# Last batch of a two-layer mixture: seven block products instead of eight for the second layer too, on two units at once

## The chip, the core and the metric

One core of one Trainium2 chip runs the kernel. The metric is device time of a whole execution in microseconds (us); the median of three runs of the kernel before is 1190.45 us (1190.12 to 1192.12). TensorE (PE) multiplies, VectorE (DVE), ScalarE (ACT) and GpSimd (POOL) do the element work, SyncE (SP) and ScalarE issue the DMAs used here. [...]

## The reference, cut to what matters

```python
scores = q @ k.T / sqrt(D)                 # 4 batches, 8 heads, 768 rows, D = 64
scores += -slope[h] * dist                 # local window of n_local = 96 and n_global = 8 first columns
a = softmax(where(keep, scores, -1e9)) ; x = a @ v      # x: 3072 rows x 512
p = domain_probs / domain_probs.sum(-1)    # 4 domains
for e in range(4):
    h = maximum(x @ w1[e], 0)              # 512 -> 1024
    out += p[:, e:e+1] * (h @ w2[e])       # 1024 -> 512
```

## The kernel before

A batch is 768 rows (six tiles of 128, or two halves of 384). The hidden columns of the four domains are cut into units of 256: `units` (line 700) lists (batch, domain, group), 16 units a batch, 64 in all. Each fp32 operand is kept as two fp32r parts, a high part (a ScalarE copy) and a low part (the value minus the high part), and each product is three matmuls: high by high, high by low, low by high.

For each unit `first(i)` (line 815) makes the hidden values. The product of w1 with x is done by seven products of 2 x 2 blocks (Strassen in Winograd's form): `product` (line 782) issues six matmuls of 384 columns into one PSUM bank of the pool `ps_mm` (four banks). VectorE adds the partial sums, ScalarE does relu and writes the high part of h, and VectorE writes the low part. `second(i)` (line 876) multiplies h with w2: for each of six row tiles six matmuls of 512 columns into one bank, then one VectorE instruction weights the tile with the mixture's probability and adds it to `acc`. At the last unit of a batch ScalarE's queue sends `acc` out.

The order of a batch (from line 944) is first(0), then first(i), second(i-1) for each i, and at last second(15). Attention for the next batch (`attention`) is put between these as steps, so that its last steps end ahead of the batch's last second but one; the blocks of the next x (`blocks`, line 607) are then made by ScalarE, VectorE and GpSimd beside the following products. The last batch has no attention beside it. `load_w1` and `load_w2` (lines 720, 760) run as chores: in batch 0 they load raw weights, make the block sums and both parts with GpSimd and ScalarE and keep them in device memory; in later batches SP's queue fetches the parts back, two buffers each.

From line 941 the order is written out by hand up to a few steps into batch 0 (`Ordered.on`, class at line 30). After that the program's planner places each engine's instructions by its own estimate of their times, with program order as priority; each engine executes its own list in order.

Of the kernel before, what the change touches and what calls it, by code (L numbers as in the profile page):

```python
# [2 lines left out]

# [22 lines left out]
def f32(ap):  # L26
    return ap.bitcast(F32)
# [159 lines left out]
def attn_moe_kernel(ctx: ExitStack, tc, q, k, v, n_global, n_local, domain_probs, w1, w2, out):  # L187
# [9 lines left out]
    HALF = S // 2  # L197
    TPH = HALF // P
    SCALE = 1.0 / math.sqrt(D)

    const = ctx.enter_context(tc.tile_pool(name="const", bufs=1))
    ident = const.tile([P, P], F32, name="ident")
# [2 lines left out]
    ng = load_int(nc, const, n_global, "ng")  # L205

    main = ctx.enter_context(ExitStack())
    ve, ac, po, sy, te = (Ordered(tc, e) for e in (nc.vector, nc.scalar, nc.gpsimd, nc.sync, nc.tensor))

    PAIRS = (0, 2, 1, 3)  # L210
# [7 lines left out]
    HELDSTEPS = 14  # L218

    PL = P + NGLOB  # L220
    fast = main.enter_context(tc.tile_pool(name="fast", bufs=1))

# [48 lines left out]
    NT = N // P  # L271
    prob = const.tile([P, NT, E], F32, name="prob")

    xp = main.enter_context(tc.tile_pool(name="xp", bufs=1))
    wp = main.enter_context(tc.tile_pool(name="wp", bufs=2))
    rp = main.enter_context(tc.tile_pool(name="rp", bufs=1))

    class Pools:


        def __init__(self, stack, name, st, kd, qd, nat, natv, pb, ps, pt, px, early):
            self.early = early

            def sbuf(part, bufs):
                return stack.enter_context(tc.tile_pool(name=f"{name}_{part}", bufs=bufs))
# [427 lines left out]
            sy.dma_start(f32(kept[key]), f32(dst))  # L713

    def fetch(name, key, shape, view):
        dst = wp.tile(shape, F32R, name=name)
        sy.dma_start(f32(dst), f32(kept[key]))
        return view(dst)

# [39 lines left out]

    def load_w2(i, lead=7):  # L760

        if i >= len(units):
            return
        b, e, g = units[i]
# [7 lines left out]
        dst = wp.tile([P, 2, 2, DM], F32R, name="w2s")  # L772
# [5 lines left out]
        waiting[(i, 2)] = (e, g, 2), dst  # L778

    hs = {}  # L780

# [147 lines left out]
        mix = mixture()  # L929
        next(mix)  # L930
    Ordered.on = False
    hp = main.enter_context(tc.tile_pool(name="hp", bufs=2))
    op = main.enter_context(tc.tile_pool(name="op", bufs=1))
    ps_mm = main.enter_context(tc.tile_pool(name="ps_mm", bufs=4, space=PSUM))
    A = Pools(main, "att", st=1, kd=1, qd=1, nat=1, natv=1, pb=2, ps=2, pt=2, px=0, early=False)

    per = E * NPR
    count, span = NPAIR * (6 + NQT) + 5, (13 * per - 12) * 0.97  # L940
    Ordered.on = True
    chores.append(last)
    work_chores()
    for b in range(B):
        att = attention(b + 1, A) if b + 1 < B else iter(())
        emitted = done = 0
        begin = ONSTEPS if b == 0 else 0
        events = [(first, b * per)]
        for i in range(b * per + 1, (b + 1) * per):
            events += [(first, i), (second, i - 1)]  # L950
        events.append((second, (b + 1) * per - 1))
        for n, (fn, i) in enumerate(events):
            if n == len(events) - 2 and b + 1 < B:
                for _ in att:
                    pass
                chores.append(blocks(b + 1))
            if b == 0 and n == 0:
                chores += [load_w2(1, 12), load_w1(2, 6, 3)]
            else:
                chores.append(load_w1(i + 2, 9) if fn is first else load_w2(i + 2))  # L960
            for _ in fn(i):
                work_chores()
                done += 1
                if b == 0 and done == ONSTEPS:
                    next(mix, None)
                    next(att)
                    Ordered.on = False
                    po.held = True
                if b == 0 and done == HELDSTEPS:
                    po.held = False  # L970
                while emitted < count and emitted * (span - begin) < (done - begin) * count:
                    next(att, None)
                    emitted += 1

    main.close()


# [39 lines left out]
```

## Time and profile before

| | |
|---|---|
| median of three runs | 1190.45 us |
| span of the profiled execution (the page gives its span alone) | 1189.2 us |
| TensorE matmul / VectorE / ScalarE / GpSimd busy | 1164.3 / 825.8 / 494.4 / 210.7 us |
| batch 0, 1, 2, 3 by TensorE's order | 85 to 345, to 625, to 919, to 1184 us |

Busy time of an engine is the union of its records. [...] In the time order one line merges neighbouring instructions of one kind: start, length from the first start to the last end, engine, operation, tiles, shape and count; in brackets the idle time ahead and what ended it.

### The profile page before, as it was taken

How to read it: one execution, taken by the hardware profiler on the slowest of the kernel's cores; microseconds unless marked ns; L12 is line 12 of the kernel's file. 1: busy time of each engine (PE TensorE's matmuls, PEld its weight loads, DVE VectorE, ACT ScalarE, POOL GpSimd, SP SyncE). 2: the span in 40 equal slices, each digit the busy share in tenths (PEclk: the TensorE clock that was granted, in tenths of full speed). 3: DMA queues.
4: the chain of work that ended last, by engine and by line, in shares of the span. 5: the costliest groups of instructions: out<-in, count | busy, mean ns of one | idle time of the engine just before them, and what ended most of it. 6: DMA issues, size and time to landing. Idle time of an engine off the chain costs nothing.

```text
span 1189.2 us, 18091 instructions
## 1 busy us (share of the span) xinstructions
PE 1164.3 (98%) x6624; PEld 1039.9 (87%) x6624; DVE 825.8 (69%) x1859; ACT 494.4 (42%) x1268; POOL 210.7 (18%) x221
## 2 busy tenths in 40 slices
PE   7789999999999999999999999999999999999998
PEld 5579899898989898998988998989988999999996
DVE  7887676776687666666758867666666766666665
ACT  7955655565533444444432444444444211111110
POOL 4755665555230000000001000000001000000000
PEclk9999999999999999999999999999999999999999
DMA  8486897878578566666657657575654645554532
GB/s 200 160 246 243 306 299 264 258 278 298 178 244 275 186 209 198 201 217 213 183 178 242 237 198 219 164 238 192 206 186 154 234 188 195 195 187 177 186 133 91
DMA packets 122703, 251.38 MB, mean 211 GB/s; under 512 B 83184, under 2 KB 91376, under 8 KB 106224
## 3 DMA queue, kind: packets, MB, share of 16 engines
q1 hardware_dynamic: 118864, 243.87, 61.8%
q10 hardware_dynamic: 3744, 6.30, 1.4%
q8 instruction: 54, 0.88, 0.3%
q14 instruction: 41, 0.34, 0.1%
HBM read 174.11 MB, written 52.43 MB: 190 GB/s over the span
## 4 chain that ended last, share of the span: by engine, by line
PE 90%; DMA 3%; ACT 3%; DVE 2%; POOL 1%; issue 1%; SPq 0%; POOLq 0%; DVEq 0%
PE pm L43 80%; PE pt L43 6%; PE ps L43 3%; DMA qd<-st_q 2%; ACT pb L43 1%; DVE pb L43 1%; DMA raw<-in_moe_w_dram 1%; POOL w1s L43 0%; DMA q<-in_q_dram 0%; ACT xT L43 0%; ACT pT L43 0%; SPq L43 0%; DVE x L43 0%; ACT w1s L43 0%; POOL w2s L43 0%
## 5 line engine op out<-in xcount | busy, mean ns | idle before, releaser
L43 PE MATMUL pm<-w2s,h 128*128 128x512 f32 x2304 | 551.6, 393 | 1.5 <-DVE h L43 1.5
L43 PEld LDWEIGHTS pm<-w2s,h 128*128 128x128 f32 x2304 | 426.1, 188 | 89.4 <-DVE h L43 3.1
L43 DVE SCALAR_TENSOR_TENSOR acc<-pm,prob,acc 128x512 f32<-128x512 f32 x360 | 267.8, 749 | 151.6 <-PE pm L43 149.7
L43 PE MATMUL pm<-xT,w1s 128*128 128x384 f32 x1536 | 296.0, 337 | 1.7 <-DVE vv L43 1.0
L43 PEld LDWEIGHTS pm<-xT,w1s 128*128 128x128 f32 x1536 | 266.3, 188 | 5.2 <-issue 1.7
L43 PE MATMUL pm<-xB,w1s 128*128 128x384 f32 x1146 | 225.2, 338 | 0.2 <-DVE xB L43 0.2
L43 PEld LDWEIGHTS pm<-xB,w1s 128*128 128x128 f32 x1146 | 200.4, 188 | 5.1 <-issue 0.5
L43 ACT ACTIVATE h<-pm 128x384 fp32r<-128x384 f32 x256 | 124.7, 491 | 176.5 <-DVE pm L43 172.8
L43 DVE SCALAR_TENSOR_TENSOR h<-pm,h 128x384 fp32r<-128x384 f32 x256 | 140.5, 551 | 10.9 <-ACT h L43 7.7
L43 ACT ACTIVATE pb<-pb,nmax 128x256 f32<-128x256 f32 (+1 forms) x192 | 93.8, 495 | 92.1 <-DVE nmax L43 91.2
L43 ACT COPY p<-pm 128x384 f32<-128x384 f32 x63 | 30.2, 479 | 185.8 <-PE pm L43 176.9
L43 POOL COPY vg<-v 32x768 f32<-32x768 f32 x16 | 13.5, 843 | 505.5 <-DMA v<-in_v_dram 440.4
L43 DVE TENSOR_TENSOR u<-pm,p 128x384 f32<-128x384 f32 x64 | 35.6, 557 | 71.2 <-PE pm L43 58.1
L43 DVE CUSTOM_DVE_ANT_0 pb<-ps,nbias 128x256 f32<-128x256 f32 (+1 forms) x192 | 71.5, 396 | 8.3 <-PE ps L43 4.8
L43 ACT COPY pT<-pt 128x512 f32<-128x512 f32 (+1 forms) x96 | 53.4, 556 | 53.6 <-PE pt L43 53.4
L43 DVE TENSOR_TENSOR pm<-pm,vv 128x384 f32<-128x384 f32 x128 | 71.6, 560 | 1.5 <-PE pm L43 1.3
L43 ACT ACTIVATE pb<-pb,zsum 128x256 f32<-128x256 f32 (+1 forms) x144 | 63.3, 484 | 17.9 <-DVE zsum L43 17.8
L43 PE MATMUL pt<-ident,pb 128*128 128x128 f32 x352 | 57.4, 278 | 7.7 <-DVE pb L43 5.4
L43 PEld LDWEIGHTS pt<-ident,pb 128*128 128x128 f32 x352 | 42.1, 141 | 17.8 <-ACT pb L43 3.3
L43 DVE TENSOR_TENSOR vv<-pm,u 128x384 f32<-128x384 f32 x64 | 35.6, 557 | 27.3 <-PE pm L43 26.9
L43 DVE TENSOR_TENSOR u<-pm,u 128x384 f32<-128x384 f32 x64 | 35.6, 557 | 27.1 <-PE pm L43 26.5
L43 POOL TENSOR_TENSOR w2s<-raw,w2s 128x512 fp32r<-128x512 f32 x32 | 40.9, 1293 | 44.8 <-ACT w2s L43 44.7
(91 smaller groups left out, 881.3 us busy)
## 6 DMA issues: line engine op xcount, KB each, us to landing
w1s<-kept SPq DMA_DIRECT2D x48, 1792.0 KB, 7.3
w2s<-kept SPq DMA_DIRECT2D x48, 1024.0 KB, 4.8
kept<-w1s SPq DMA_DIRECT2D x16, 1792.0 KB, 7.9
qd<-st_q SPq DMA_DIRECT2D x96, 192.0 KB, 5.0
raw<-in_moe_w_dram SPq DMA_DIRECT2D x32, 512.0 KB, 4.7
kept<-w2s SPq DMA_DIRECT2D x16, 1024.0 KB, 6.6
v<-in_v_dram SPq DMA_DIRECT2D x16, 384.0 KB, 4.0
out_dram<-acc ACTq DMA_DIRECT2D x24, 256.0 KB, 3.4
```

The source lines that it names most:

```text
L43: ins = fn(*args, **kwargs)
```

## The change

In the last batch alone the products with w2 are done by seven products of blocks as well. Two units (the pair i, i+1 of one domain) are taken together: the contraction of 512 is two blocks of 256 (one 128-column block from each unit), the 512 output columns are two blocks of 256, the rows are two halves of 384. A product is 18 matmuls of 256 columns: three row tiles, two units, three parts. The partial sums of a pair stay in six PSUM banks, X and Y for three row tiles, into whose halves products are added by TensorE, and VectorE adds between them (`behind`). Two banks (`psF`) are left for the w1 products.

`first_late` makes hidden values as whole fp32 blocks in SBUF (`hf`), without high and low parts; `sum_values` (GpSimd) makes four sums of these blocks, and `split_value` (ScalarE and VectorE) and `split_sum` (ScalarE and GpSimd) write the parts. In `period` each of the seven w2 products of a pair is followed by two w1 products of the pair after it; `last_period` has w2 products alone. All of this stands in program order. The first unit's w1 products of the last batch move ahead of the last w2 products of batch 2.

The four sums of w2's blocks (T1 to T4) are made once for each (domain, group) by the chore `load_t` in batches 1 and 2 and kept in device memory. Pools that end before the last batch stand on the other side of SBUF (`mid`), so that the new pools can take their place.

```diff
@@ load_w2: returns for the last batch; w2s comes from its own pool wp2
+    def load_t(e, g, lead=6):
+        raw = rp.tile([P, 2, DM], F32, name="raw2")
+        sy.held = True
+        sy.dma_start(raw, w2[e, g * 2 * P : (g + 1) * 2 * P, :].rearrange("(a p) m -> p a m", p=P))
+        sy.held = False
+        for _ in range(lead):
+            yield 1
+        b11, b12, b21, b22 = (raw[:, f, s] for f in range(2) for s in (slice(0, HM), slice(HM, DM)))
+        low = rp.tile([P, 4, 2, P], F32, name="sums").rearrange("p n a f -> p n (a f)")
+        high = rp.tile([P, KT, 2 * P], F32, name="raw1")
+        po.tensor_sub(low[:, 0], b12, b11)
...
+        ac.copy(high.bitcast(F32R), low)
+        yield 1
+        po.tensor_tensor(low.bitcast(F32R), low, high, op=ALU.subtract)
+        for _ in range(4):
+            yield 1
+        dst = kept[(e, g, 3)] = dp.tile([4, P, 2, HM], F32R, name=f"kept_{e}_{g}_3")
+        for n, src in enumerate((high, low)):
+            ac.dma_start(f32(dst[:, :, n, :]).rearrange("n p m -> p n m"), src)
@@ after the start
+    SLOTS = (
+        ("P1", "A11", "B11", 0, 0), ("P2", "A12", "B21", 0, 0), ("P6", "S2", "T2", 1, 0), ("P5", "S1", "T1", 0, 1),
+        ("P7", "S3", "T3", 1, 1), ("P3", "S4", "B22", 0, 1), ("P4", "A22", "T4", 1, 0),
+    )
+    def first_late(i):
+        def prod(a, x):
+            return product(i, a, x, lt["psF"].tile([P, 512], F32, name="pf"))[:, :HALF]
+        def last(name, pm, other):
+            ve.tensor_add(pm, pm, other)
+            ac.activation(hf[:, HBLOCKS.index(name)], pm, AF.Relu)
+        ac.copy(p1, prod("A11", "B11"))
+        yield
+        last("A11", prod("A12", "B21"), p1)
+        yield
+        ve.tensor_add(u, prod("S2", "T2"), p1)
+        yield
+        ve.tensor_add(vv, prod("S1", "T1"), u)
+        yield
+        pm = prod("S3", "T3")
+        ve.tensor_add(u, pm, u)
+        last("A22", pm, vv)
+        yield
+        last("A12", prod("A22", "T4"), u)
+        yield
+        last("A21", prod("S4", "B22"), vv)
+        yield
+    def halves(eng, dst, k, src):
+        ac.copy(dst[:, 0, k], src)
+        eng.tensor_tensor(dst[:, 1, k], src, f32(dst[:, 0, k]), op=ALU.subtract)
+    def sum_values(i, eng=po):
+        eng.tensor_add(s1, a21, a22)
+        eng.tensor_sub(s2, s1, a11)
+        po.tensor_sub(s4, a12, s2)
+        po.tensor_sub(s3, a11, a21)
+        def big(G, s, pm):
+            for t in range(TPH):
+                n = 0
+                for k in range(2):
+                    for hi, wi in ((0, 0), (1, 0), (0, 1)):
+                        te.matmul(
+                            pm[low][t][:, cols], blk[a][:, hi, k, t * P : (t + 1) * P], w[:, k, wi, :],
+                            start=(n == 0 and name in ("P1", "P6", "P5")), stop=(n == 5), skip_group_check=True,
+                        )
+                        n += 1
+                yield
+            load_late()
+        def behind(s, t, pm, saved, other):
+            X, Y = pm[0][t], pm[1][t]
+            if s == 0:
+                ac.copy(saved[t], X[:, left])
+            elif s == 2:
+                ve.tensor_add(saved[t], Y[:, left], saved[t])
+            elif s == 3:
+                ve.tensor_add(X[:, right], X[:, right], saved[t])
+                ac.copy(other[t], X[:, right])
+            elif s == 4:
+                ve.tensor_add(Y[:, left], Y[:, right], saved[t])
+                ve.tensor_add(Y[:, right], Y[:, right], other[t])
+        def period(G, before):
+            for s in range(7):
+                for _ in big(G, s, pm):
+                    pass
+                if s == 0:
+                    split_value("A12", i + 1)
+                    split_value("A22", i, True)
+                    sum_values(i + 1)
+                    if before:
+                        mix(G - 1, before[1], 3)
+                        mix(G - 1, before[1], 4)
+                elif s == 1:
+                    split_sum("S2", i + 1)
+                    split_sum("S1", i + 1)
+                    if before:
+                        mix(G - 1, before[1], 5)
+                    split_value("A22", i + 1)
+                    split_value("A11", j, True)
...
+                elif s == 6:
+                    split_sum("S3", j, True)
+                    split_sum("S4", j, True)
+                    for t in range(TPH):
+                        mix(G, pm[0], t)
+                for t in range(TPH):
+                    behind(s, t, pm, saved, other)
+                next(more)
+                if final and s == 6:
+                    mix(G, pm[1], 3)
+                next(more)
+        def last_period(G, before):
...
+            for t, _ in enumerate(big(G, 2, pm)):
+                behind(2, t, pm, saved, other)
+            for t in range(TPH):
+                mix(G, X, t, 0)
+            for t, _ in enumerate(big(G, 3, pm)):
+                behind(3, t, pm, saved, other)
...
@@ the loop over batches
-    for b in range(B):
+    for b in range(B - 1):
...
+        tail = b == B - 2
+        if tail:
+            events.append((first_late, (b + 1) * per))
         events.append((second, (b + 1) * per - 1))
...
+            if b in (1, 2) and fn is first and i % 2 == b - 1:
+                chores.append(load_t(*units[i][1:]))
...
+    Ordered.on = True
+    mid.close()
+    late_batch()
```

## Rows read from the trace of the kernel before

**Rows 1.** The page: span, busy time of each engine (share of the span) and instructions, and TensorE's granted clock in tenths for 40 equal slices.
```profile
span 1189.2 us, 18091 instructions
PE 1164.3 (98%) x6624; PEld 1039.9 (87%) x6624; DVE 825.8 (69%) x1859; ACT 494.4 (42%) x1268; POOL 210.7 (18%) x221
PEclk9999999999999999999999999999999999999999
```

**Rows 2.** Busy time by stage: the start's end, batches 0, 1, 2 and 3. Columns: window, its length, busy time of each engine and instructions, granted clock, share of the DMA engines' time, GB/s.
```profile
core 0: us, PE busy (x) PEld busy (x) DVE busy (x) ACT busy (x) POOL busy (x), PEclk, DMA share, GB/s
60.00:85.00 25.00, 21.72 (x130) 18.02 (x129) 20.42 (x47) 14.51 (x32) 14.91 (x15) 1.00 0.76 208
85.00:345.00 260.00, 259.52 (x1507) 233.99 (x1506) 180.10 (x390) 149.90 (x377) 140.51 (x139) 1.00 0.78 270
345.00:625.00 280.00, 279.05 (x1609) 252.01 (x1608) 192.52 (x416) 114.67 (x302) 3.30 (x4) 1.00 0.64 206
625.00:919.00 294.00, 293.29 (x1685) 264.94 (x1685) 207.02 (x438) 123.25 (x318) 10.55 (x8) 1.00 0.62 203
919.00:1189.00 270.00, 264.43 (x1320) 238.20 (x1319) 177.77 (x293) 41.98 (x84) 2.85 (x2) 0.99 0.49 177
```

**Rows 3.** The last link of the chain that ended last (start, length, engine, tile, count), and from the table of waits of 919 to 1189 us, TensorE's only row (in total, times, longest).
```profile
918.78 264.67 PE pm L43 x1320
...
PE pm L43 <- DVE h L43: 0.3, 1, 0.3
```

**Rows 4.** TensorE in order of time in the last batch, one unit.
```profile
980.83 8.36 PE L43 MATMUL pm<-w2s,h 128*128 128x512 f32 x36
989.03 1.23 PE L43 MATMUL pm<-xB,w1s 128*128 128x384 f32 x6
990.10 3.28 PE L43 MATMUL pm<-xT,w1s 128*128 128x384 f32 x18
993.22 2.24 PE L43 MATMUL pm<-xB,w1s 128*128 128x384 f32 x12
```

**Rows 5.** TensorE in order of time in batch 1, with attention's scores (256 columns) and transposes (128 columns) between; then the weight loads of the scores grouped by form.
```profile
402.01 0.64 PE L43 MATMUL ps<-kd,qd 128*128 128x256 f32 x4
402.48 1.21 PE L43 MATMUL pm<-xT,w1s 128*128 128x384 f32 x6
...
406.65 0.64 PE L43 MATMUL ps<-kd,qd 128*128 128x256 f32 x4
407.12 0.60 PE L43 MATMUL pt<-ident,pb 128*128 128x128 f32 x4
407.48 4.81 PE L43 MATMUL pm<-w2s,h 128*128 128x512 f32 x20
...
L43 PEld LDWEIGHTS ps<-kd,qd 128*128 128x128 f32 x288 | 43.9, 188 | 4.9 <-issue 1.2 <-DMA qd<-st_q 0.9
```

**Rows 6.** Groups of instructions over the span, kept apart by form: busy us, mean ns of one, idle before them.
```profile
L43 DVE SCALAR_TENSOR_TENSOR acc<-pm,prob,acc 128x512 f32<-128x512 f32 x360 | 267.8, 749 | 151.6 <-PE pm L43 149.7
L43 ACT ACTIVATE h<-pm 128x384 fp32r<-128x384 f32 x256 | 124.7, 491 | 176.5 <-DVE pm L43 172.8
L43 DVE CUSTOM_DVE_ANT_0 pb<-ps,nbias 128x256 f32<-128x256 f32 x160 | 63.2, 418 | 6.3 <-PE pt L43 3.5 <-PE ps L43 2.8
L43 POOL TENSOR_TENSOR w2s<-raw,w2s 128x512 fp32r<-128x512 f32 x32 | 40.9, 1293 | 44.8 <-ACT w2s L43 44.7
L43 DVE TENSOR_TENSOR vv<-pm,u 128x384 f32<-128x384 f32 x64 | 35.6, 557 | 27.3 <-PE pm L43 26.9
L43 POOL TENSOR_TENSOR sums<-raw 128x256 f32<-128x256 f32 x32 | 23.5, 751 | 37.4 <-DMA raw<-in_moe_w_dram 37.3
L43 ACT COPY pT<-pt 128x256 f32<-128x256 f32 x16 | 6.0, 372 | 0.3 <-PE pt L43 0.3
L43 POOL TENSOR_TENSOR xB<-x,xB 128x384 fp32r<-128x384 f32 x4 | 4.0, 1002 | 1.0 <-ACT xB L43 1.0
L43 ACT CAST xT<-x 128x384 fp32r<-128x384 f32 x8 | 3.9, 512 | 2.4 <-DVE x L43 2.4
L43 DVE TENSOR_TENSOR xT<-x,xT 128x384 fp32r<-128x384 f32 x3 | 1.7, 559 | 1.3 <-ACT xT L43 1.2
```

**Rows 7.** VectorE and GpSimd in order of time at the end of batch 1: a split of 768 columns by VectorE beside two by GpSimd. The same split by VectorE alone is the last of [rows 9].
```profile
631.38 2.63 DVE L43 TENSOR_TENSOR xT<-x,xT 128x768 fp32r<-128x768 f32 x1
...
629.57 3.64 POOL L43 TENSOR_TENSOR xB<-x,xB 128x768 fp32r<-128x768 f32 x2
```

**Rows 8.** DMA issues: count, KB each, median us from issue to landing.
```profile
w1s<-kept SPq DMA_DIRECT2D x48, 1792.0 KB, 7.3
w2s<-kept SPq DMA_DIRECT2D x48, 1024.0 KB, 4.8
```

**Rows 9.** TensorE and VectorE in order of time at the start of the last batch.
```profile
918.78 16.62 PE L43 MATMUL pm<-w2s,h 128*128 128x512 f32 x72 [0.28 <-DVE h L43]
935.23 1.23 PE L43 MATMUL pm<-xB,w1s 128*128 128x384 f32 x6
...
926.30 0.94 DVE L43 TENSOR_TENSOR xT<-x,xT 128x768 fp32r<-128x768 f32 x1
927.17 2.21 DVE L43 SCALAR_TENSOR_TENSOR acc<-pm,prob,acc 128x512 f32<-128x512 f32 x3
929.30 0.95 DVE L43 TENSOR_TENSOR xT<-x,xT 128x768 fp32r<-128x768 f32 x1
```

**Rows 10.** The end: VectorE's last instruction.
```profile
1183.47 0.75 DVE L43 SCALAR_TENSOR_TENSOR acc<-pm,prob,acc 128x512 f32<-128x512 f32 x1 [0.61 <-PE pm L43]
```

More of the change, by code (lines that the diff above doesn't have):

```diff
@@ L2 @@
 from contextlib import ExitStack
+from functools import partial
 import concourse.bass as bass
@@ L220, in attn_moe_kernel @@
     PL = P + NGLOB
-    fast = main.enter_context(tc.tile_pool(name="fast", bufs=1))
+    fast = mid.enter_context(tc.tile_pool(name="fast", bufs=1, side="right"))
     nbias = fast.tile([P, H, 3 * P], BF16, name="nbias")
@@ L715, in fetch @@
     def fetch(name, key, shape, view):
-        dst = wp.tile(shape, F32R, name=name)
+        dst = (wp if name == "w1s" else wp2).tile(shape, F32R, name=name)
         sy.dma_start(f32(dst), f32(kept[key]))
@@ L760, in load_w2 @@
     def load_w2(i, lead=7):
-        if i >= len(units):
+        b, e, g = units[i]
+        if b == B - 1:
             return
-        b, e, g = units[i]
         if b > 0:
@@ L771, in load_w2 @@
             yield 1
-        dst = wp.tile([P, 2, 2, DM], F32R, name="w2s")
+        dst = wp2.tile([P, 2, 2, DM], F32R, name="w2s")
         wts[(i, 2)] = dst
@@ L931, in attn_moe_kernel @@
     Ordered.on = False
-    hp = main.enter_context(tc.tile_pool(name="hp", bufs=2))
     op = main.enter_context(tc.tile_pool(name="op", bufs=1))
-    ps_mm = main.enter_context(tc.tile_pool(name="ps_mm", bufs=4, space=PSUM))
-    A = Pools(main, "att", st=1, kd=1, qd=1, nat=1, natv=1, pb=2, ps=2, pt=2, px=0, early=False)
+    hp = mid.enter_context(tc.tile_pool(name="hp", bufs=2, side="right"))
+    ps_mm = mid.enter_context(tc.tile_pool(name="ps_mm", bufs=4, space=PSUM, side="right"))
+    att_stack = mid.enter_context(ExitStack())
@@ new lines, in attn_moe_kernel @@
+    A = Pools(
+        att_stack, "att", st=1, kd=1, qd=1, nat=1, natv=1, pb=2, ps=2, pt=2, px=0, early=False, side="right"
+    )
[3 more added lines that the diff above has]
+    )
+    PLAIN = {"B11": (0, 0), "B12": (0, 1), "B21": (1, 0), "B22": (1, 1)}
+    SUMS = ("S1", "S2", "S3", "S4")
+    HBLOCKS = ("A11", "A12", "A21", "A22")
@@ new lines, in attn_moe_kernel, with open_late @@
+    lt, hfs, sfs, blk = {}, {}, {}, {}
+    def open_late():
+        lt["hf"] = main.enter_context(tc.tile_pool(name="hf", bufs=2))
+        lt["blk"] = main.enter_context(tc.tile_pool(name="blk", bufs=1))
+        lt["psF"] = main.enter_context(tc.tile_pool(name="psF", bufs=2, space=PSUM))
+    def first_late(i):
+        hf = hfs[i] = lt["hf"].tile([P, 4, HALF], F32, name="hf")
+        p1, u, vv = sums_of_products()
+        def prod(a, x):
[19 more added lines that the diff above has]
+        yield
@@ new lines, in block, with split_value, split_sum @@
+    def block(name, fresh):
+        if fresh:
+            blk[name] = lt["late" if name in ("S3", "S4", "A22") else "blk"].tile([P, 2, 2, HALF], F32R, name=f"h{name}")
+        return blk[name]
+    def halves(eng, dst, k, src):
+        ac.copy(dst[:, 0, k], src)
+        eng.tensor_tensor(dst[:, 1, k], src, f32(dst[:, 0, k]), op=ALU.subtract)
+    def split_value(name, i, fresh=False):
+        halves(ve, block(name, fresh), i % 2, hfs[i][:, HBLOCKS.index(name)])
+    def split_sum(name, i, fresh=False, eng=po):
+        halves(eng, block(name, fresh), i % 2, sfs[i][:, SUMS.index(name)])
@@ L956, in attn_moe_kernel @@
                 chores.append(blocks(b + 1))
+                if tail:
+                    att_stack.close()
+                    open_late()
             if b == 0 and n == 0:
@@ L959, in attn_moe_kernel @@
             else:
-                chores.append(load_w1(i + 2, 9) if fn is first else load_w2(i + 2))
+                if fn is not first_late:
+                    chores.append(load_w2(i + 2) if fn is second else load_w1(i + 2, 9))
+            if b in (1, 2) and fn is first and i % 2 == b - 1:
+                chores.append(load_t(*units[i][1:]))
             for _ in fn(i):
@@ L973, in attn_moe_kernel @@
                     emitted += 1
+    work_chores()
+    for _ in load_w1((B - 1) * per + 2):
+        pass
+    Ordered.on = True
+    mid.close()
+    late_batch()
     main.close()
```

132 lines of the change are left out of this document (127 added, 5 removed).

## The prediction

> **What bounds the kernel now.** I read the page's busy shares and clock first, then busy time by stage, then the chain of waits with the table of who waited for whom, and last the order of time. [...] The last batch begins in the chain at 918.78 and is one unbroken run of 1320 matmuls; TensorE waited there once, for 0.3 us [rows 3]. VectorE is busy 178 of 270 us there, ScalarE 42, GpSimd 3, and the DMA engines have half their time free [rows 2]. So in that stage only the number and spacing of matmuls count, as long as nothing else is late. The reader should see the spacing in [rows 4]: from one row's start to the next, 36 matmuls of 512 columns take 8.20 us (227.8 ns each) and 18 of 384 columns take 3.12 us (173.3 ns). The recorded durations (0.39 and 0.33 us) overlap and are no measure.
>
> The profile's span is 1189.2 us; the median of the timed runs, 1190.45, lies 1.25 us above. I work on the span and add 1.25.
>
> **1. Products with w2: fewer columns.** Before, 16 units x 36 matmuls of 512 columns = 576 x 0.2278 = 131.2 us. After, 8 pairs x 7 products x 3 row tiles x 6 matmuls = 1008 of 256 columns. The trace has such matmuls in the attention scores, same types and a new 128x128 weight each: four starts in 0.47 us, twice, 117.5 ns each [rows 5]. The two other widths differ by 54.5 ns per 128 columns, which extrapolates to 118.8 ns for 256. I take 118.8: 1008 x 0.1188 = 119.8 us, so **-11.4 us** (117.5 gives -12.8). The bound from the other side: a weight load's record is 188 ns long [rows 5], and loads that could not overlap would give 189.5 us (+58); but in the bursts loads of that record follow at 117.5 ns, and four transposes with a load each start within 0.36 us, so I keep nothing of that end except in a rival. Bursts of four are shorter than the 18 that follow here; that is the doubt that stays.
>
> [...]
>
> **2. The steady period.** One period is seven slots: a product with w2 (18 matmuls, 2.14 us), then two w1 products of the units after next (12 x 0.1733 = 2.08 us): 4.2 us a slot, 29.5 us a period. Loads of the engines, with durations from [rows 6]: VectorE 14 sums of 0.56, 6 splits of 0.56, 12 adds of 256 columns (not shown as adds; the 128x256 form from PSUM took 0.42), 6 mixtures of 0.75: 7.8 + 3.4 + 5.0 + 4.5 = 20.7 us. ScalarE 8 relu and 2 copies of 0.49, 14 splits of 0.51, 6 copies of 256 columns (0.37): 14.3. GpSimd 8 sums and 8 splits of 384 columns, 1.0 each: 16. All fit in 29.5, so none becomes the bound by sum. What counts is chains in order.
> - The tightest: A21 of a pair's second unit is the last product of a period. Recorded end +0.2, VectorE's sum 0.56, relu 0.49: 1.3 us into the next period. GpSimd then makes s1, s2, s4, s3 until 5.5. ScalarE's copy of S2 stands behind the relu of slot 0's second product (ends 4.2, +0.2 +0.56 +0.49), so 5.5 to 6.0; GpSimd's low part ends at 7.0. P6 wants it at 8.4 (low part at 8.9). Slack some 1.5 to 2 us.
> - P2 adds into the bank that ScalarE copies after P1: two w1 products (2.08 us) cover three copies of 0.37 and two splits. P1 of the next period needs the bank X that three mixtures (2.25 us) read in slot 6; they end about 0.5 us ahead of it.
> - Against this speaks a pair of rows: VectorE's split of 768 columns took 0.95 us alone [rows 9], but 2.63 when it began at 631.38 while GpSimd was in the middle of a pair of tensor operations on SBUF (629.57 to 633.21, one ending near 631.4, the next near 633.2) [rows 7]: it waited one whole GpSimd operation. The six VectorE splits and 16 GpSimd operations of a period meet; each meeting costs up to 1.0 us, and two splits (A12, A22) stand exactly beside s1 and s2 in the tight chain. Two waits of 1.0 use up the slack. So a stall between 0 and 0.9 us a period; I take 0.2, since one meeting is still covered: 7 x 0.2 = **+1.4** (0 to 6).
>
> [...]
>
> **3. The prologue.** After the last old product with w2, seven w1 products of unit 49 run back to back with two PSUM banks instead of four. A bank must come free in the 1.04 us of the next product. Its release takes 0.2 + 0.56 (VectorE) + 0.1 + 0.49 (relu) = 1.35 for most, over by 0.3; for A22, with two sums, 1.9, over by 0.85; and one VectorE split (0.55) stands ahead of one of the sums. Sum **+1.7** (bounds: 0 if other work fills it; 4 if the memory of the closed pools, freed only with the last old matmul, also delays the first w2 loads, which need 4.8 us before [rows 8] and have some 9).
>
> **4. The boundary.** The first w1 products of the last batch move ahead by one unit. Blocks of x were made beside 72 matmuls from 918.78 to 935.23 [rows 9], VectorE finishing the last at 930.25; now the products may start after 36, at 927. In their order T1 and T4 are wanted at about 930 and 932, so data are just in time, but VectorE also has the mixtures, and there are two banks again. Where a product is late the planner may put matmuls of the neighbour unit there. Bounds -0.5 and +3; I take **+1.0**.
>
> **5. The last period.** No w1 products lie between. P5 writes the bank X that VectorE first mixes: after P6's last tile 0.2 + 0.42 (add) + 0.42 (mixture) + issue, 1.2 us on TensorE; P2 behind ScalarE's copy 0.3: **+1.5** (0.5 to 4). At the very end the last mixture has 256 instead of 512 columns: 0.75 becomes 0.42 [rows 6, 10]: **-0.3**.
>
> **6. Preparing the sums of w2 in batches 1 and 2.** 16 times: four GpSimd subtractions (0.75 each), one of 1024 columns (about 2.6, twice the 1.29 of 512), a ScalarE copy (about 1.1), two DMA issues on ScalarE's queue and 1.5 MB moved. Batch 0 is the cover's proof: there GpSimd worked 140 and ScalarE 150 of 260 us at 270 GB/s, and TensorE still had 259.5 busy [rows 2]. The stores wait on ScalarE's queue for GpSimd, and relu and exp stand behind them. Bounds 0 and +4; I take **+0.5**. Loads in the last batch become 7 x 0.5 + 2 x 1.75 = 7 MB a period, 240 GB/s, under batch 0's 270; five buffers give 20 us for a load that took 4.8 to 7.3 [rows 8]: 0. The queue is SP's, in order; each w2 load waits for a product already done when it is issued, so w1 behind it isn't held.
>
> **Sum.** -11.4 + 1.4 + 1.7 + 1.0 + 1.5 - 0.3 + 0.5 = -5.6: span 1183.6, time **1184.9 us**.
>
> **Rivals.**
> - *All covered.* The stalls of 2 to 6 vanish, as batch 0 hid everything: -11.7, 1178.8 us. For it: no gap of TensorE in three batches. Against: two banks instead of four, and no w1 work in the last period.
> [...]
> - *The chain of sums takes TensorE's place* in each period, at P6: GpSimd's s1 to S2 with every VectorE split ahead of one of them. With a stall of s us a period the time is 1183.5 + 7s. At s = 1.0 nothing is gained (1190.5); from s = 1.34 it is slower by 0.2%. That needs the chain 3 us longer than worked out, three full meetings, or GpSimd 40% slower than its rows. For: [rows 7]; against: the slack of 1.5 us. At s between 0.6 and 1.3: about 1190. At 1.6: 1195, slower.
> - *Weight loads bound the 256-column stream.* At the burst's end 117.5 holds; if a long stream ran at 135 ns, 16 us go and the change costs 11 over all: 1201. Against: the bursts show no growth between first and fourth.
>
> **Chances.** Forecast 0.56 (its own range 1181 to 1188), all covered 0.12, page's gap 0.03, chain with no gain 0.17, chain slower 0.08, weight loads 0.04. About 0.2% (2.4 us) is what can be told from no change. Faster 0.71, same 0.17, slower 0.12. The range 1180 to 1192 leaves out the two best cases in part and the slower ones.
>
> **What would show it.** Starts of 256-column matmuls at 117 to 120 ns inside a product (step 1); TensorE waiting for S2 or A12 once a period (2), for ScalarE or VectorE releasing pf tiles near the beginning of the batch (3, 4), for VectorE on X at P5 at the end (5); batches 1 and 2 as long as before within 1 us (6). The forecast is wrong if the spacing is over 125 ns, or if the gaps inside the periods sum to more than 6 us.

## The result and the profile after

The changed kernel takes 1205.05 us (median of 4 runs, 1202.86 to 1207.92), the kernel before beside it 1191.01 (1190.12 to 1192.12). The ratio is 1.0121, 95% interval 1.0104 to 1.0139: slower by 1.2%, where 1184.9 us was forecast and 1180 to 1192 was the range.

The page of the kernel after, span and busy times; they answer to [rows 1]:

```profile
span 1202.2 us, 19701 instructions
...
PE 1163.2 (97%) x7056; PEld 1055.3 (88%) x7056; DVE 835.8 (70%) x1900; ACT 568.0 (47%) x1444; POOL 431.1 (36%) x426
```

Busy time by stage of the kernel after, with the columns of [rows 2]:

```profile
85.00:345.00 260.00, 258.76 (x1505) 233.66 (x1505) 180.63 (x392) 151.43 (x380) 139.89 (x139) 1.00 0.81 269
345.00:625.00 280.00, 274.26 (x1551) 246.16 (x1550) 188.82 (x410) 119.23 (x306) 39.47 (x39) 0.99 0.75 240
625.00:919.00 294.00, 291.63 (x1666) 262.06 (x1665) 200.40 (x430) 125.28 (x319) 50.79 (x47) 1.00 0.77 249
919.00:1201.00 282.00, 269.52 (x1836) 262.11 (x1835) 198.90 (x348) 109.13 (x254) 147.46 (x133) 0.99 0.64 224
```

The line to stop at is the second. From 345 to 625 us TensorE was idle 280 - 274.26 = 5.7 us, where it had been idle 0.95 [rows 2], and it issued 1551 matmuls instead of 1609. Batch 1 holds none of the new products; what is new in it is the preparation of the sums of w2.

For the balance I cut both traces at the same matmuls: the start of the first matmul with w2, and the starts of the last matmul with w2 of units 15, 31 and 46:

| stage, us | before | after | difference |
|---|---|---|---|
| start | 84.1 | 85.8 | +1.7 |
| batch 0 | 273.2 | 272.8 | -0.4 |
| batch 1 | 289.4 | 298.3 | **+8.9** |
| batch 2, to unit 46 | 280.2 | 283.8 | **+3.6** |
| from unit 46 to the last matmul | 256.2 | 252.6 | -3.6 |
| last matmul to the end | 6.2 | 8.8 | +2.6 |

The last stage did gain. The loss is in batches 1 and 2, in which every product is as it was, and 2.6 us are lost behind the last matmul. The start is the same program in all kernels of this study but one, and lies between 84.1 and 87.3 us in their profiles, so I count its +1.7 as spread.

**Where batch 1 stops.** In the table of waits of the kernel after (total, times, longest), the first two rows are TensorE's from 345 to 919 us, the third is ScalarE's from 345 to 925:

```profile
PE pm L44 <- DVE h L44: 3.5, 4, 1.7
PE pt L44 <- ACT pT L44: 2.1, 1, 2.1
...
ACT raw L44 <- POOL sums L44: 35.7, 15, 6.1
```

ScalarE stood 35.7 us, 15 times, in front of one copy, `raw <- sums`, and waited for GpSimd's `sums`. That is the copy of `load_t`. The longest stop of TensorE, the one in the second row, shows what that does, in order of time (SPq and ACTq are the issues of DMAs):

```profile
553.35 0.60 PE L44 MATMUL pt<-ident,pb 128*128 128x128 f32 x4
...
554.71 1.43 POOL L44 TENSOR_TENSOR sums<-raw 128x256 f32<-128x256 f32 x2 [31.76 <-DMA raw<-in_moe_w_dram]
...
556.11 1.65 POOL L44 TENSOR_TENSOR sums<-raw,sums 128x256 f32<-128x256 f32 x2
...
557.79 1.04 ACT L44 CAST raw<-sums 128x1024 fp32r<-128x1024 f32 x1 [3.28 <-POOL sums L44]
558.86 0.59 ACT L44 COPY pT<-pt 128x512 f32<-128x512 f32 x1
...
558.92 2.36 POOL L44 TENSOR_TENSOR sums<-sums,raw 128x1024 fp32r<-128x1024 f32 x1 [1.16 <-ACT raw L44]
...
559.50 1.02 PE L44 MATMUL pt<-ident,pb 128*128 128x128 f32 x4 [2.10 <-ACT pT L44]
...
561.31 0.37 ACTq L44 DMA_DIRECT2D kept<-sums  x1
561.72 0.59 ACT L44 COPY pT<-pt 128x512 f32<-128x512 f32 x1 [1.88 <-POOL sums L44]
```

Read it from the top, as a knot of three engines. Attention's transposes end at 553.95 and their bank is to be emptied by ScalarE's `pT` copy. That copy stands behind `raw <- sums` in ScalarE's list, which idles 3.28 us until GpSimd ends its four subtractions at 557.76. So `pT` runs at 558.86 instead of about 554.5, and TensorE's next transposes, which want the bank, begin at 559.50 after 2.10 us of nothing. At 561.31 it happens once more: the store of the low part has to wait for GpSimd's 2.36 us operation (end 561.28), and the next `pT` copy with it, 1.88 us.

The stops for `h` in the first row I followed for the longest alone, 1.73 us at 451.07. It goes back to a store of the low part:

```profile
443.61 2.40 POOL L44 TENSOR_TENSOR sums<-sums,raw 128x1024 fp32r<-128x1024 f32 x1 [1.17 <-ACT raw L44]
...
446.04 0.37 ACTq L44 DMA_DIRECT2D kept<-sums  x1
...
447.44 1.12 DVE L44 TENSOR_TENSOR kd<-pt,kd 64x384 fp32r<-64x384 f32 x2 [1.74 <-ACT kd L44]
...
451.07 3.26 PE L44 MATMUL pm<-w2s,h 128*128 128x512 f32 x13 [1.73 <-DVE h L44]
```

GpSimd ends at 446.01 and the store goes out; ScalarE's work for `kd` follows it, VectorE has idled 1.74 us for that, and VectorE's sums for `h` stand behind `kd`.

In the first knot GpSimd itself had waited for the raw load: it is one of two in the kernel's chain of waits (start, length) that took longest:

```profile
544.64 9.94 DMA raw<-in_moe_w_dram
...
783.18 10.39 DMA raw<-in_moe_w_dram
```

The first ends at 554.58, 0.13 us ahead of the four subtractions. Both were issued on SP's queue 0.4 us behind w1's load of 1792 KB (544.22 and 782.80).

The stop costs more than its length. Windows around it, columns as above, granted clock the third from the end:

```profile
552.00:559.50 7.50, 5.41 (x34) 4.89 (x32) 3.13 (x5) 2.63 (x5) 3.55 (x5) 1.00 0.87 235
559.50:563.10 3.60, 3.60 (x13) 3.60 (x14) 1.73 (x4) 0.92 (x2) 1.77 (x1) 0.53 1.19 289
563.10:570.00 6.90, 6.90 (x54) 6.22 (x54) 5.28 (x14) 3.81 (x11) 0.00 (x0) 1.00 0.62 207
```

Behind the pause the granted clock was 0.53 over these 3.6 us, and 1.00 before and after them; 3.6 x (1 - 0.53) = 1.7 us of work are lost to it. Of the 12.5 us of the two batches, the idle time between TensorE's records accounts for 6.5 (8.1 against 1.7 over 345 to 919) and the clock for 1.7. The other 4 do not show as idle time, since a matmul's record reaches some 0.16 us past the next one's start (in [rows 4], 980.83 + 8.36 against 989.03). By the spacing of starts about 1 of them belongs to the recorded pauses (ten against four), which are longer than their records say, and most of the rest to spacings that are a tenth of a us or so too long (156 against 131); I did not place these one by one.

### The profile page after: what moved, and what is told of

Read it like the earlier page. It is cut to its first block, busy times and chain, and to the rows that moved or that the text cites. A ratio compares the mean times of both kernels' runs of the same rounds, so it can differ in the third digit from the quotient of the medians.

```text
span 1202.2 us, 19701 instructions
## 1 busy us (share of the span) xinstructions
PE 1163.2 (97%) x7056; PEld 1055.3 (88%) x7056; DVE 835.8 (70%) x1900; ACT 568.0 (47%) x1444; POOL 431.1 (36%) x426
## 4 chain that ended last, share of the span: by engine, by line
PE 78%; DMA 7%; ACT 4%; DVE 4%; POOL 3%; issue 2%; SPq 1%; ACTq 0%; DVEq 0%; POOLq 0%
PE pm L44 51%; PE pf L44 9%; PE pt L44 6%; DMA raw<-in_moe_w_dram 5%; PE X L44 5%; PE Y L44 4%; PE ps L44 3%; POOL sums L44 2%; DMA qd<-st_q 1%; ACT pb L44 1%; SPq L44 1%; DVE pb L44 0%; ACT pT L44 0%; DVE acc L44 0%; DVE u L44 0%
## 5 line engine op out<-in xcount | busy, mean ns | idle before, releaser
L44 PE MATMUL pm<-w2s,h 128*128 128x512 f32 x1728 | 419.3, 394 | 4.9 <-DVE h L44 4.7
L44 PEld LDWEIGHTS pm<-w2s,h 128*128 128x128 f32 x1728 | 317.6, 188 | 71.6 <-DVE h L44 7.8
L44 DVE SCALAR_TENSOR_TENSOR acc<-pm,prob,acc 128x512 f32<-128x512 f32 x270 | 200.2, 748 | 101.7 <-PE pm L44 99.9
L44 PE MATMUL pm<-xT,w1s 128*128 128x384 f32 x1152 | 225.7, 340 | 2.0 <-DVE vv L44 0.8
L44 PEld LDWEIGHTS pm<-xT,w1s 128*128 128x128 f32 x1152 | 200.2, 189 | 5.6 <-issue 1.5
L44 PE MATMUL pm<-xB,w1s 128*128 128x384 f32 x858 | 169.7, 339 | 0.8 <-ACT x L44 0.6
L44 PEld LDWEIGHTS pm<-xB,w1s 128*128 128x128 f32 x858 | 149.9, 189 | 4.9 <-ACT x L44 0.8
L44 POOL TENSOR_TENSOR hS<-sf,hS 128x384 fp32r<-128x384 f32 x63 | 67.6, 1093 | 63.0 <-ACT hS L44 62.9
L44 PE MATMUL pf<-xT,w1s 128*128 128x384 f32 x384 | 74.2, 337 | 3.4 <-ACT hf L44 2.6
L44 PEld LDWEIGHTS pf<-xT,w1s 128*128 128x128 f32 x384 | 65.5, 188 | 5.3 <-ACT hf L44 3.3
L44 PEld LDWEIGHTS pt<-ident,pb 128*128 128x128 f32 x352 | 42.5, 142 | 20.8 <-ACT pb L44 3.7
```

The source lines that it names most:

```text
L44: ins = fn(*args, **kwargs)
```

## The experiments

Three explanations were open for the loss in batches 1 and 2: ScalarE's list waits for GpSimd and holds attention back (the queue); the stores and loads crowd the kernel's other transfers (the traffic); or the loss has nothing to do with the preparation and comes from the other order and places of the changed program. The expectations below were written ahead of each run. "Stages" are batch 1, and batch 2 up to the products with w2 of unit 45: 289.4 and 264.1 us before, 298.3 and 267.5 after.

**No preparation.** `load_t` is left out, and the four products that would read T1 to T4 read plain blocks of w2.

```diff
-                chores.append(load_t(*units[i][1:]))
...
-    src = kept[(e, g, 3)][BLOCKS2.index(name)]
+    f, half = divmod(BLOCKS2.index(name), 2)
+    src = kept[(e, g, 2)][:, :, f, half * HM : (half + 1) * HM]
```

> The changed kernel with no preparation of the four sums of w2 in batches 1 and 2 (no loads, no GpSimd, ScalarE or store for them); the last batch reads plain blocks of w2 in their place, so the four products with T blocks use other numbers. Batch 1 to 2 (second unit 15's last matmul to unit 31's) took 289.4 us before and 298.3 after, batch 2 (to unit 45's) 264.1 and 267.5. Theory 1 (the preparation makes TensorE late): 289 to 290 and 264 to 265, time 1191 to 1194. Theory 2 (the planner's order moved because of the new pools, whatever the chore): both stay long, 297 and 267, time 1203 to 1206. Theory 3 (the time went in the last batch): batches as after, time unchanged.

1189.18 us, ratio to before 0.9984 (0.9975 to 0.9994). Stages 288.2 and 264.0: the loss is gone. From unit 46 to the last matmul 250.7. Its windows:

```profile
345.00:625.00 280.00, 279.89 (x1613) 252.72 (x1612) 195.09 (x417) 113.92 (x302) 4.15 (x4) 1.00 0.66 209
625.00:919.00 294.00, 293.54 (x1689) 265.69 (x1688) 205.87 (x436) 122.78 (x316) 9.80 (x8) 1.00 0.63 204
```

**The preparation alone**, `load_t` and its call, put into the kernel before; the last batch is the old one and the sums are not used.

```diff
...
+            if b in (1, 2) and fn is first and i % 2 == b - 1:
+                chores.append(load_t(*units[i][1:]))
```

> The kernel before with the preparation of the sums added as the change has it, and nothing else of the change; what it stores is not read. Theory 1: batches 1 and 2 grow as they did after, 8 and 3 us, time 1200 to 1204. Theory 2 (pools and planner, not the chore): 1191 to 1193.

1203.36 us, ratio 1.0099 (1.0078 to 1.0119); stages 297.1 and 268.6, so +7.7 and +4.5. The two runs agree from both sides: the preparation alone costs some 12 us, and nothing else in the change makes these batches longer.

**The stores on SP's queue.**

```diff
-            ac.dma_start(f32(dst[:, :, n, :])...
+            sy.dma_start(f32(dst[:, :, n, :])...
```

> The changed kernel with the two stores of each preparation issued on SP's queue, not on ScalarE's. DMA traffic is the same. Theory 1a (ScalarE's queue is held by the store that waits for GpSimd's low part, 1.9 to 2.0 us each of 16 times): about half of the loss goes, batch 1 293 to 295, time 1198 to 1201. Theory 1b (ScalarE is held by the copy that waits for GpSimd's four subtractions): batch 1 stays 297 to 299. Theory 4 (the extra DMA traffic is what slows): nothing goes, 1203 to 1206; SP held by the stores instead could make it worse.

1202.2 us, ratio 1.01 (1.0083 to 1.0117); stages 295.6 and 266.3. ScalarE still waited 41.5 us in front of the copy (15 times, longest 6.0). So the stores are the smaller part, about 3 of the 14 us by the medians; the two intervals (1.0083 to 1.0117 here, 1.0104 to 1.0139 for the change) overlap, so that even this is not clear of the spread.

**ScalarE out of the preparation altogether**: GpSimd makes the high part too, and SP's queue has the stores (the GpSimd version below).

```diff
-        ac.copy(high.bitcast(F32R), low)
+        po.tensor_copy(high.bitcast(F32R), low)
...
-            ac.dma_start(f32(dst[:, :, n, :])...
+            sy.dma_start(f32(dst[:, :, n, :])...
```

> The changed kernel with the preparation made by GpSimd alone (its copy makes the high part) and its stores on SP's queue: ScalarE does nothing for it, traffic is the same. Theory 1 (ScalarE's queue is held): batch 1 289 to 291, batch 2 264 to 266, time 1192 to 1195. Theory 4 (traffic): batch 1 296 to 298, time 1202 to 1206.

1191.89 us, ratio 1.0005 (0.9992 to 1.0018); stages 291.7 and 264.0. The same bytes are moved, by the same number of DMAs, and GpSimd does more work, yet 10 of the 12 us are back in these stages (555.7 us together, 565.8 after, 553.5 before). Its windows beside those of the kernel after show that the traffic is the same, 249 and 244 GB/s against 240 and 249:

```profile
345.00:625.00 280.00, 279.94 (x1616) 253.03 (x1614) 194.20 (x418) 114.56 (x302) 50.88 (x51) 1.00 0.78 249
625.00:919.00 294.00, 291.91 (x1669) 263.41 (x1669) 205.96 (x431) 120.34 (x312) 56.19 (x50) 0.99 0.75 244
```

The traffic falls as the main cause, and so does GpSimd's load: together they can have no more than the 3.5 us by which these stages are still longer than without the preparation (555.7 against 552.2). One stop of 1.85 us is left in it, at the end of batch 1:

```profile
624.76 2.38 POOL L44 TENSOR_TENSOR sums<-sums,raw 128x1024 fp32r<-128x1024 f32 x1
624.86 3.10 DVE L44 TENSOR_TENSOR xB<-x,xB 128x768 fp32r<-128x768 f32 x1
...
632.09 8.24 PE L44 MATMUL pm<-w2s,h 128*128 128x512 f32 x28 [1.85 <-DVE h L44]
```

VectorE's split, 0.95 us alone [rows 9], took 3.10 beside GpSimd's long operation and ended 0.82 us after it (624.76 + 2.38 = 627.14, 624.86 + 3.10 = 627.96); VectorE's sums for h stand behind it, and h is late. It is what [rows 7] showed, now on the path. The 0.82 is close to the 0.95 that the split takes alone; that VectorE stood still until GpSimd's operation had ended is my reading of these times.

**The wait or the work?** The GpSimd version took two things from ScalarE: its work, 1.04 us of copying and two DMA issues a preparation, and its wait. A first try to part them puts the copy and the stores of the changed kernel later:

```diff
-        yield 1
-        yield 1
+        for _ in range(6):
+            yield 1
         ac.copy(high.bitcast(F32R), low)
         yield 1
         po.tensor_tensor(low.bitcast(F32R), low, high, op=ALU.subtract)
-        for _ in range(4):
+        for _ in range(8):
```

> The changed kernel with ScalarE's work for the sums as it is (16 copies of 1.05 us, 32 store issues), but its copy stands four steps and its stores four steps further behind GpSimd's instructions in program order. Theory 1c (it is ScalarE's waiting, in the order of its queue, that costs): most of the loss of batches 1 and 2 goes, time 1192 to 1197. Theory 1d (it is ScalarE's own work, 1.8 us a time): it stays, 1201 to 1206.

1202.63 us, ratio 1.0103 (1.0088 to 1.0117); stages 298.1 and 264.5. The edit did not do what it was for: ScalarE waited for `sums` 35.9 us, 15 times, as without the edit. Batch 2 recovered and batch 1 did not; by this run the question stays open. It does show that the sum of the waits alone does not fix the price: what stands behind each of them counts too.

A second try adds to the GpSimd version two ScalarE copies of 1024 columns a preparation, with no wait in them:

```diff
...
+        for _ in range(2):
+            ac.copy(fast.tile([P, 1024], F32, name="idle"), nbias...[:, :1024])
```

> GpSimd alone prepares the sums (1191.9), and ScalarE makes two copies of 1024 columns for each preparation from a table that is always ready into a place that nobody reads: 2.1 us of work a time, more than the change gave it (1.05 and two issues of 0.37), and nothing to wait for. Theory 1c (its waiting costs, not its work): 1191 to 1194, batches 1 and 2 at 290 to 292 and 264 to 265. Theory 1d (its work costs): 1200 to 1206.

1197.55 us, ratio 1.0062 (1.0047 to 1.0076). Stages 290.2 and 264.2, but the copies were not in them: as their input is there from the beginning, the planner moved all 32 to between 20.8 and 134.2 us, and the start grew to 89.4 us. It is no test.

The next two, on the GpSimd version too, belong together. One has the same work tied to its place, by an input that exists only then (h of the unit before); the other has next to no work, but waits: one column of `sums` is copied after the subtractions, and once more behind the stores.

```diff
+        ready = f32(hs[i - 1][:, 0])...[:, :1024]
+        for _ in range(2):
+            ac.copy(fast.tile([P, 1024], F32, name="idle"), ready)
```

> GpSimd alone prepares the sums (1191.9), and beside each preparation ScalarE makes two copies of 1024 columns (2.1 us) of the high part of the unit before's h, which ScalarE itself wrote, into a place that nobody reads: more work than the change gave it (1.8 us), no wait for another engine, and bound to batches 1 and 2 (the copies of the run before, from a table, all stood before 135 us). Theory 1c (waiting costs): batches 1 and 2 at 290 to 293 and 264 to 266, time 1191 to 1194. Theory 1d (work costs): 296 to 298 and 266 to 268, time 1200 to 1205.

```diff
+        ac.copy(fast.tile([P, 1], F32, name="idle"), low[:, 3, 0:1])
...
+        ac.copy(fast.tile([P, 1], F32, name="idle"), low[:, 3, 0:1])
```

> GpSimd alone prepares the sums (1191.9), and ScalarE copies one column twice for each preparation: once what GpSimd's four subtractions wrote, at the place of the change's copy, once the low part at the place of the change's stores. Under 0.3 us of work a time, and the change's two waits. Theory 1c (waiting costs): batches 1 and 2 at 295 to 299 and 266 to 268, time 1199 to 1205. Theory 1d (work costs): 290 to 292 and 264 to 265, time 1191 to 1194.

Work without a wait: 1191.67 us, ratio 1.001 (1.0 to 1.002), stages 291.1 and 264.4, the same as without it. A wait with hardly any work: 1209.75 us, ratio 1.0152 (1.0135 to 1.0169), stages 298.5 and 272.4. The instructions added, by the view of their tile (count, duration in ns at least, median and at most, first and last start, form), first with the work:

```profile
L44 ACT COPY idle<-h x32: 1033/1050/1062, 343.9 to 906.7; 128x1024 f32<-128x1024 f32 x32
```

then with the wait, and below it the idle time of ScalarE ahead of them:

```profile
L44 ACT COPY idle<-sums x32: 191/192/194, 381.4 to 955.5; 128x1 f32<-128x1 f32 x32
...
  POOL sums L44: 83.1, 32
```

Against the GpSimd version (1191.89) 32 copies of 1.05 us cost nothing that can be told from no change, and 32 of 0.19 us that wait cost 18 us. The same place in order of time, with the wait:

```profile
560.16 0.19 ACT L44 COPY idle<-sums 128x1 f32<-128x1 f32 x1 [3.31 <-POOL sums L44]
...
560.37 0.59 ACT L44 COPY pT<-pt 128x512 f32<-128x512 f32 x1
...
561.01 0.55 PE L44 MATMUL pt<-ident,q 128*128 128x128 f32 x3 [1.59 <-ACT pT L44]
```

It is the knot of the kernel after, tied by a 0.19 us instruction. That settles it for the larger part of the loss: the wait at the head of ScalarE's list is the cost, not what ScalarE does there. No row here shows ScalarE passing a waiting instruction: above, `pT` starts 0.02 us behind the end of the copy that waited 3.31 us (560.16 + 0.19, then 560.37).

**The tail.** On the GpSimd version the outputs of the last period are sent in halves, each as soon as its columns are done:

```diff
+            def send(eng, r, half):
+                r0, cols = b * S + r * P, slice(half * HM, (half + 1) * HM)
+                eng.dma_start(out[r0 : r0 + P, cols], accs[(b, r)][:, cols])
...
                 mix(G, X, t, 0)
+                send(sy, t, 0)
...
                 mix(G, Y, TPH + t, 1)
+                send(sy, TPH + t, 1)
...
-                    (sy if t % 2 else ac).dma_start(out[r0 : r0 + P, :], accs[(b, r)])
+                    send(sy if t % 2 else ac, r, 1 - low)
```

> The kernel of the experiment in which GpSimd alone prepares the sums (1191.9), and in the last period each half of 256 columns of an output tile is sent as soon as it is final, so that only 0.8 MB instead of 1.5 MB leave after the last two products. Theory 5 (the end is long because six whole tiles of 256 KB are issued within 2 us and share the DMA engines): last matmul to end of span falls from 8.1 to 8.8 us to some 6.5, time 1189.5 to 1190.5. Theory 6 (the end is set by issue and landing of the very last transfer, whatever its company): stays over 8, time as without it.

1191.04 us, ratio 1.0003 (0.9995 to 1.0012). Last matmul to the end: 7.3 us, against 8.8 in the kernel after, 8.1 in the run it is built on and 6.2 before. 6.5 had been expected. The runs whose last period is that of the kernel after lie between 8.1 and 8.8 us, the three later ones with halves between 7.6 and 7.9. So the bunching of outputs is at most a part of the tail's loss, and the other 1 to 2 us stay open.

**All repairs together, and the preparation elsewhere.** On top of the halves: three of the prologue's products use banks of the still unused Y, the last period's X mixtures go ahead of its sums and the Y mixtures directly behind each tile's sums, and the preparation runs once a unit in the first half of a batch.

```diff
-            if b in (1, 2) and fn is first and i % 2 == b - 1:
-                chores.append(load_t(*units[i][1:]))
+            if b in (1, 2) and fn is first and 1 <= i % per <= per // 2:
+                chores.append(load_t(*units[i - 1 + (b - 1) * (per // 2)][1:]))
...
-        more = firsts([begin + 1])
+        more = firsts([begin + 1], (None, None, "Y0", "Y1", "Y2", None, None))
```

> The last one with three more edits: the preparation of the sums runs in units 1 to 8 of batches 1 and 2 (once a unit) and not in the later ones, off the boundary where x's blocks are split; in the seven products ahead of the first period three use banks of X and Y's pool that are still free; in the last period VectorE mixes the left half of X ahead of its adds on Y, and Y's right halves behind each tile's adds. By my reading of the traces: boundary stall of 2.0 us and the clock's fall behind it go (3 us), the 2.4 us ahead of the first period shrink to 1, the 1.6 us of the last period to 0.5: 1184 to 1187. If the stalls are elsewhere made up for: 1189 to 1191.

1195.4 us, ratio 1.0037 (1.0025 to 1.0049). From unit 46 to the last matmul 246.9 us (252.6 after, 256.2 before), the best so far; but stages 292.7 and 271.4. The waits of its batches 1 and 2 have one row, for attention's loads:

```profile
PE ps L44 <- DMA qd<-st_q: 7.2, 3, 3.1
```

In two of the three stops (at 441.7 and 735.8 us) these loads are issued directly behind a store of the sums on SP's queue, and the last of them, behind w1's and the raw load as well, lands 10.6 and 10.3 us after its issue. In the third no store stands ahead of them. That the closer spacing of the preparations fills the queue is therefore my reading and not shown, though the next run, which widens it again, loses only 0.6 us to these loads.

**The same with the preparation in every second unit again:**

```diff
-            if b in (1, 2) and fn is first and 1 <= i % per <= per // 2:
-                chores.append(load_t(*units[i - 1 + (b - 1) * (per // 2)][1:]))
+            if b in (1, 2) and fn is first and i % 2 == b - 1:
+                chores.append(load_t(*units[i][1:]))
```

> The kernel with all edits, but the preparation back at one for every two units, as in the change (GpSimd alone, stores on SP's queue). In the kernel with one a unit the last batch took 254.5 us from unit 46's end to the end (262.4 before, 258.8 with GpSimd alone), and its batches 1 and 2 lost 10 us at waits for attention's loads (2.2, 3.2 and 2.3 us). If the two parts add: batch 1 290 to 292, batch 2 264, span 1184, time 1185 to 1187. If the last batch's gain is taken up by what stands ahead of it: 1189 to 1191.

1188.14 us (1186.43 to 1189.41), ratio 0.9977 (0.9968 to 0.9986). Stages 291.0 and 263.9, unit 46 to the last matmul 246.9, tail 7.9. It beats both kernels; the one before, 1190.7 us beside it, by 0.23%.

**Its stores on GpSimd's queue**, against the waits of SP's:

```diff
-            sy.dma_start(f32(dst[:, :, n, :])...
+            po.dma_start(f32(dst[:, :, n, :])...
```

> The same, with the stores of the sums on GpSimd's own queue, so that no other engine's queue holds an instruction that waits for GpSimd. If SP's waits (some 56 us in all for the sums) still make loads late: batch 1 289 to 290, 1 to 2 us faster than with SP's queue. If not: the same time within 1 us, or slower if GpSimd's issuing holds its splits at the boundary.

1191.28 us, ratio 1.0007 (0.9996 to 1.0018); stages 290.6 and 265.6, nothing gained there. New is a late first load of w2 in the last batch:

```profile
PE X L44 <- DMA w2b<-kept: 2.9, 2, 2.2
```

## Why the prediction was wrong

**Step 6 failed.** It sized the preparation at +0.5 with a bound of +4; it measured +8.9 and +3.6 in its own stages, +12.2 when put in alone, and 1.9 more where the last one fell on the boundary (unit 46 to the last matmul 252.6, without it 250.7). The sign that the step gave itself, batches 1 and 2 as long as before within 1 us, is the one that failed. No rival had it: the 0.12 for slower stood on the chain of sums and on the weight loads, and neither came. The step did name the mechanism, "the stores wait on ScalarE's queue for GpSimd, and relu and exp stand behind them", but priced it by the engines' busy shares and took batch 0 as "the cover's proof". That proof does not carry, and the trace of before had the number that says so, in a group that was not read for it:

```profile
L43 ACT CAST w1s<-sums 128x512 fp32r<-128x512 f32 x32 | 19.5, 628 | 4.6 <-POOL sums L43 4.5
```

In batch 0 and the start ahead of it (38.5 to 325 us) ScalarE made 32 high parts of GpSimd's sums and idled 4.6 us for them in all, 0.14 each; the 15 copies of 1024 columns in batches 1 and 2 idled 35.7, 2.4 each. Busy time was alike, the wait was not. Two terms were left out. The copy itself waits, not the stores alone: most raw loads of the preparations land 8 to 10 us after their issue, four subtractions follow in a row, and the copy stands in ScalarE's list as if it were ready sooner. And what stands behind it is on TensorE's path: an engine idle for more than half of the time (ScalarE was busy 119.23 of 280 us in batch 1) has no slack left where TensorE wants its bank back 3.5 us after filling it (553.95 to 557.41) and 3.28 of them pass in a wait. Why the planner put the copy just there was not tried further than by the run that moved it later.

**The tail was mis-sized**: -0.3 forecast, +2.6 measured. The step, part of the fifth, looked at the last mixture only. It is shorter, as said, but three of 256 columns come in a burst now. In order of time, after:

```profile
1192.38 4.07 ACTq L44 DMA_DIRECT2D out_dram<-acc  x4
1192.77 1.51 SPq L44 DMA_DIRECT2D out_dram<-acc  x2
1193.05 1.26 DVE L44 SCALAR_TENSOR_TENSOR acc<-Y,prob,acc 128x256 f32<-128x256 f32 x3
```

and before:

```profile
1177.46 7.14 ACTq L43 DMA_DIRECT2D out_dram<-acc  x6
```

Before, six outputs of 256 KB left 1.36 us apart, each behind its row tile; after, the issues of all six start within 2.0 us, and the last of them takes until 1196.45. From the last mixture's end to the span's end it is 1189.2 - 1184.22 = 5.0 us before [rows 10] and 1202.2 - 1194.31 = 7.9 after. By the landings in the traces, 3.5 and 5.1 of these lie ahead of the last output's landing, which the halves brought to 3.9; the 1.5 and 2.8 us behind it became 2.5, and what lengthens them no run tried.

**Step 1 was right.** One slot of the steady state, after:

```profile
1040.71 2.31 PE L44 MATMUL X<-w2b,hS 128*128 128x256 f32 x18
1042.86 2.25 PE L44 MATMUL pf<-xB,w1s 128*128 128x384 f32 x12
1044.94 2.31 PE L44 MATMUL Y<-w2b,hS 128*128 128x256 f32 x18
1047.09 1.21 PE L44 MATMUL pf<-xB,w1s 128*128 128x384 f32 x6
```

18 matmuls of 256 columns from 1040.71 to 1042.86 are 119.4 ns each; 118.8 was extrapolated from the two wider forms, 117.5 read from bursts of four. So 1008 x 0.1194 = 120.4 and the gain is 10.8 instead of 11.4. With it the rival of weight loads falls. A shorter gap, to which the chances give 0.03, is not in these rows.

**Step 2 was too careful**: 1.4 forecast, none measured. From 970 to 1175 us TensorE is busy 205.00 of 205 us, and the spacing of starts adds no more than 0.2. The meetings of VectorE with GpSimd do happen:

```profile
L44 DVE TENSOR_TENSOR hA<-hf,hA 128x384 fp32r<-128x384 f32 x46 | 42.0, 937 | 31.7 <-ACT hA L44 31.7
```

a split takes 937 ns on average where 559 was the mean before [rows 6], but the slack of the chain takes it all. The rival in which the chain of sums becomes the bound falls with that.

**Steps 3 to 5 were near.** Prologue: stops of 0.78, 1.14 and 0.49 us by the spacing of starts, 2.4 in all, forecast 1.7. Boundary: 2.2 in the kernel after, but 0.5 without the preparation; forecast 1.0. Last period: 0.91 and 0.41 idle in the records, 1.6 by the spacing; forecast 1.5. Loads in the last batch ran at 240 GB/s, as worked out, and none was waited for. Taken together, steps 1 to 5 ahead of the tail said -5.8 from unit 46 on; without the preparation it was 250.7 - 256.2 = -5.5. That this lies within 0.3 is in part luck: the stall of step 2 that did not come (1.4) makes up for 0.6 less gain in step 1 and 0.7 more in the prologue.

So the account of the last batch held, and the change would have been worth some 2 us net of its tail (1189.18 against 1190.86 beside it), had it not paid 12 to 14 us in batches whose products it does not touch.

## What to carry to other kernels

An instruction put into the list of an engine that serves others cost its wait here, not its duration (32 copies of 0.19 us that waited cost 18 us, 32 of 1.05 us that did not wait cost nothing that can be told from no change): ask what must have happened when it reaches the head, the landing of its data behind the largest load of the queue included (most raw loads took 8 to 10 us here), and who stands behind it. A chain of preparation that waits for loads belonged here on an engine that nobody else waits for, whole: the same copy took 1.05 us on ScalarE and 1.04 on GpSimd, and moving it to GpSimd gave back 10 us (1202.2 to 1191.89). A busy share below a half, 119.23 of 280 us in batch 1, proved no cover, and neither did another stage with other work behind the same wait.

## What the runs showed that was not expected

- 32 waits of ScalarE, 83.1 us in all ahead of 0.19 us copies, cost 18 us of the kernel's time, a little over a fifth of their length.
- Once in batches 1 and 2 of the kernel after (559.5 to 563.1) and once in the GpSimd version (from 632.9, for 3.4 us) a pause of TensorE of about 2 us was followed by a granted clock of about half: 0.53 over the 3.6 us in the kernel after, and in the GpSimd version 28 matmuls of 512 columns from 632.09 took 8.24 us, where 36 take 8.36 in [rows 4]. In the kernel after two other pauses of 1.7 us (ending at 451.07 and 950.05) were not, the clock behind them was 1.00, nor was the same stop in the preparation alone (2.0 us), nor pauses of 1.9 and 2.0 us with the stores on SP's queue, with 1.00 over both batches in these two runs. The length of the pause alone does not tell which is.
- A load of 512 KB of raw weights landed in 5.9 us by the median of all 48 issues of the kernel after, but the 16 of the preparations took 5.4 to 10.4, all but one of them over 7.7; 13 of the 16 were issued 0.4 us behind w1's load. In the GpSimd version they landed as late (6.4 to 10.1), with ScalarE not waiting for them.
- Of the 12.5 us, some 4 lie where the records of TensorE show no idle time; a balance by equal matmuls finds them, one by busy time does not.
